# Clustered attention, PReLU FFN and routed experts: output copies, routing steps and attention's first scores put elsewhere

## The chip, the cores and the metric

The kernel runs on one core of one Trainium2 chip. The metric is the device time of one execution in microseconds (us). Five engines work beside each other, each with its own in-order instruction queue: TensorE (matmuls; its weight loads are listed apart), VectorE, ScalarE, GpSimd, and SyncE, which here only issues DMAs. In the rows they are PE (PEld for the weight loads), DVE, ACT, POOL and SP (SPq for SP's issues).

## The reference, cut to what matters

Three stages, all in float32:

```
# attention: batch 2, 8 heads, 768 positions, head size 64, 16 clusters per head
q_assign, k_assign = argmax over clusters of normalised q, k times normalised centroids
scores = where(q_assign == k_assign, q @ k.T / 8, -1e9);  attn = softmax(scores);  x = attn @ v
# FFN on 1536 rows of 512, hidden size 2048
h = x @ w_in;  g = max(h, 0) + alpha * min(h, 0);  y = g @ w_out
# experts: 8 of them, hidden size 1024, rows with y @ w_skip <= 0 pass through
e = argmax(y @ w_gate);  out = y + softmax(y @ w_gate)[e] * (max(y @ w1[e], 0) @ w2[e])
```

## The kernel before

**Precision.** Each float32 operand is held as a high part (a cast to fp32r) and a low part (the rest), and a product is made of three matmuls: high by high, low by high, high by low. So each stage has casts on ScalarE for the high part and subtractions on VectorE or GpSimd for the low part.

**Attention** (`attention`) goes through 8 pairs of heads; each head has 6 steps of 128 query rows, so step i belongs to head i // 6 and pair i // 12, and k = i % 12 is the step within the pair. A step makes 128x768 scores in a PSUM tile `s` (two of them, `ps_s`), takes the maximum (VectorE, `highest`), the exponential (ScalarE, `expo`), the transposes and the product with v two and more steps later. The order of the work in a step is written out by hand (`ORD`), and every engine runs its instructions in that order. The scores are two accumulated matmuls of 128 rows per half: AB holds (q high, q low) stacked on (k high, k high), and CD holds (q high on one-hot cluster rows) on (k low on one-hot rows times 2^60), so that the mask comes out of the same matmul. AB and CD are filled by DMAs from a tile RL, which holds the four parts (1: q high, 2: k high, 0: q low, 3: k low) of both heads of a pair (`place`, L277), and by three DMAs from `st` for the one-hot rows (`placeoh`, L284). For head 0 of pair 0 ScalarE writes the one-hot rows directly into the lower 64 partitions of CD (`onehot0`, L263).

While pair n runs, pair n + 1 is prepared at fixed steps k: similarities (`sims`, L178, at k in SIM = 1, 2), the one-hot tile (`sims2`, at 3), the split into parts (`split`, at k in SP = 2, 3, on GpSimd), `place` at 6, `onehots` and `placeoh` at 8. For pair 1 the scaling of q (`scaleq`, L217) is a ScalarE instruction issued ahead of the loop, directly behind the load of the pair (L441).

At the very start matmuls on a zero tile (`busy`, counts in `WARM`) keep TensorE occupied.

**FFN** (`ffn`) works on two groups of 768 rows, gi 0 and 1 (gi is the batch), and 16 blocks of 128 hidden columns, f 0 to 15. `hiddens` makes a block in two halves c of 384 rows: 12 matmuls into a tile `h` (two buffers, `ps_h`), then PReLU, then the cast `gh` (L656) and the low part `gl` (L658). `second` (L666) multiplies a finished block into six PSUM tiles y of 128 rows; `ps_y` has six banks for the twelve tiles of both groups, so group 1's tile t takes the bank of group 0's tile t once that has been copied out (`evac`, L685: a ScalarE copy and two DMAs). TensorE's order in group 1 is: the two halves of block f, then `second` of block f - 1 for f up to 12; blocks 13 to 15 follow each other directly, and the rest of the second products comes in `tail`.

Blocks 0 and 1 of group 0 are interleaved with the last steps of attention (`blocks`, L727), with `act=True`: ScalarE makes Relu(-h) and Relu(h), VectorE adds them with the slope (L645). In group 1 ScalarE makes Relu(-h) and scales it (L650), and VectorE combines it with h in PSUM (L651). Otherwise VectorE does both (L653, L654).

Weights of the FFN come in as 64-bit words and are converted on ScalarE, VectorE and GpSimd (`Convert.word`), two blocks ahead.

**Routing.** In group 1 VectorE computes group 0's gate products (`gateb`) between the blocks. `route1` (L716: best expert, running counts per expert in `Ms`) stands in block 10, `ranks` (L935: three small matmuls that sum the counts, then positions on VectorE) in block 11, `first_tile` (L959: one-hot of the positions, then six small matmuls into a tile of `ps_h` that give the row numbers of the first expert tile) in blocks 12 and 13, and the gather of these rows behind it. `wsp.hi` and `wsp.lo` split the first experts' weights in chunks.

Of the kernel before, what the change touches and what calls it, by code (L numbers as in the profile page):

```python
# [20 lines left out]
P = 128  # L21
# [65 lines left out]
LK = 8  # L87
XB = 3
LATE = 3
WARM = (8, 3, 4, 9, 14)  # L90
PREP = (33, 45)
OK = 8
PK = 8
# [5 lines left out]
def attention(ctx, tc, A, cst, xs, conv=None, prepare=None, then=None):  # L99
# [192 lines left out]
    grp = {}  # L292
    dens = {}

    def scores(i):
        hd, t = divmod(i, NT)
        n, j = divmod(hd, 2)
        AB, CD = ABs[j], CDs[j]
        s = ps_s.tile([P, 2, 512], F32, tag="s", name="s")
        for u in range(2):  # L300
            ks = slice(u * 384, (u + 1) * 384)
            nc.tensor.matmul(s[:, u, :384], lhsT=AB[:, 0, t * P:(t + 1) * P], rhs=AB[:, 1, ks], start=True, stop=False)  # L302
        for u in range(2):
            ks = slice(u * 384, (u + 1) * 384)
            nc.tensor.matmul(s[:, u, :384], lhsT=CD[:, 0, t * P:(t + 1) * P], rhs=CD[:, 1, ks], start=False, stop=True)  # L305
        if t % 3 == 0:
            if j == 0:
                dens[n, t // 3] = wk.tile([P, 2, 3], F32, tag="den", name="den", bufs=4)
            den = dens[n, t // 3][:, j]
            eth = wk.tile([P, NT, 384], F32R, tag="eth", name="eth", bufs=2)  # L310
            etl = wk.tile([P, NT, 384], F32R, tag="etl", name="etl", bufs=2)
            grp[i // 3] = (den, eth, etl)
        es[i] = s
# [113 lines left out]
    sims(0, 1)  # L427
    busy(WARM[2])
    oq = onehot0(0)
    busy(WARM[3])  # L430
    sims2(0, (1,))
    ok = onehot0(1)
    busy(WARM[4])
    st = heads[0, "st"] = hk.tile([96, 2, 2, P], F32R, tag="st", name="st", bufs=1)
    nc.vector.tensor_copy(st[:, 0], oq[:96, 0])
    nc.vector.tensor_scalar(out=st[:, 1], in0=ok[:96, 1], scalar1=BIG, scalar2=-BIG, op0=ALU.mult, op1=ALU.add)
# [1 line left out]
    vsplit(0, 1)  # L438
    if len(seq) > 1:
        load(1)  # L440
        scaleq(1)  # L441

    def before():
        def new(n):
# [10 lines left out]
    for i in range(NI + L + 7):  # L455
        n, k = divmod(i, 12)
        m = n + 1
        if i == NI and then is not None:
            early.close()
            for _ in first:  # L460
                pass
            fill = then(wk.tile([P, 2 * DM], I32, tag="RL", name="cvt", bufs=1))
            next(fill)
        if conv is not None and i in (2, 3):
            conv.load(i - 2)
        if conv is not None and i in PREP:
            prepare(PREP.index(i))
        if i % 3 == 1 and 0 <= i - 4 < NI and (i - 4) // 3 % 4 > 1:
            recip((i - 4) // 12, (i - 4) // 3 % 2)
        gi, part = divmod(i - L - 3, 3)  # L470
        live = 0 <= gi < NI // 3
        back = 0 <= i - L < NI
        for do in ORD[i % 3]:
            if do == "S" and i < NI:
                scores(i)
            if do == "S" and k == 0 and n < len(seq):
                place(n, 1)
                placeoh(n, 1)
            if do == "M" and i < NI:
                highest(i)  # L480
            if do == "P" and live:
                pv(gi, part)
                if part == 1 and gi % 4 > 1:
                    recip2(gi // 4, gi % 2)
            if do in "AB" and back:
                transp(i - L, "AB".index(do))
            if do in "ab" and back:
                lows["ab".index(do)]()
            if do == "V" and live:
                evac(gi)  # L490
            if do == "E" and i < NI:
                expo(i)
            if do == "X" and conv is not None and CV0 <= i and (k not in CVX or i >= NI):

                next(first, None)
        if live and part == 2 and gi % 4 > 1:
            late.append((i + (LATE if i < NI else 0), gi))
        if late and late[0][0] <= i:
            gl = late.pop(0)[1]
            spare += normalize(gl // 4, gl % 2)  # L500
            while spare and i < NI:
                spare.pop(0)()
        for _ in range(FILL[max(i - NI, 0)] if i >= NI else 0):
            next(fill, None)
            if spare and i > NI + NRM:
                spare.pop(0)()
        if m < len(seq):
            if k in SIM:
                sims(m, SIM.index(k))
            if k == S2 and m == 1:  # L510
                sims2(m)
            if k in SP:
                split(m, SP.index(k))
            if k == S2 and m > 1:
                sims2(m)
            if k == 6:
                place(m, 0)
            if k == OK:
                onehots(m)
            if k == PK:  # L520
                placeoh(m, 0)
            if k == LK and m + 1 < len(seq):
                load(m + 1)
            if k == VS[0]:
                vsplit(m, 0)
            if k == VS[1]:
                vsplit(m, 1)
            if k == 11 and m + 1 < len(seq):
                scaleq(m + 1)
# [51 lines left out]
def ffn(tc, A, cst, xs, xp, y1d, R, cv, W32, fw, ps_h, cvt, more):  # L581
# [42 lines left out]
    def hiddens(gi, f, eng, after=lambda c: None, between=lambda: None, act=False, mid=lambda c: None):  # L624
        xh, xl = xs[gi]
        wh, wl = ws.pop((f, 0))
        if gi == 1 and NF - TAIL <= f < NF - 2:
            gh, gl = over["xh"].pop(0), over["xh"].pop(0)
        else:
            gh = fw.tile([P, GN], F32R, tag="gh", name="gh")  # L630
            gl = fw.tile([P, GN], F32R, tag="gl", name="gl")
        for c in range(2):
            o = slice(c * HC, (c + 1) * HC)
            h = ps_h.tile([P, HC], F32, tag="h", name="h")
            for i, (a, x) in enumerate(((wh, xh), (wh, xl), (wl, xh))):
                for k in range(KD):
                    nc.tensor.matmul(h, lhsT=a[:, k * P:(k + 1) * P], rhs=x[:, k, o], start=(k == 0 and i == 0), stop=(k == KD - 1 and i == 2))  # L637
                if i < 2:
                    yield
            m = fw.tile([P, HC], F32, tag="gm", name="gm")  # L640
            if act:
                t = fw.tile([P, HC], F32, tag="gt", name="gt", bufs=1)
                nc.scalar.activation(t, h, AF.Relu, scale=-1.0)
                nc.scalar.activation(m, h, AF.Relu)
                nc.vector.scalar_tensor_tensor(out=m, in0=t, scalar=nalpha[:, f:f + 1], in1=m, op0=ALU.mult, op1=ALU.add)  # L645
            elif gi == 1:

                t = fw.tile([P, HC], F32, tag="gt", name="gt", bufs=1)
                nc.scalar.activation(t, h, AF.Relu, scale=-1.0)
                nc.scalar.activation(t, t, AF.Copy, scale=nalpha[:, f:f + 1])  # L650
                nc.vector.scalar_tensor_tensor(out=m, in0=h, scalar=0.0, in1=t, op0=ALU.max, op1=ALU.add)  # L651
            else:
                nc.vector.tensor_scalar(out=m, in0=h, scalar1=0.0, scalar2=alpha[:, f:f + 1], op0=ALU.min, op1=ALU.mult)  # L653
                nc.vector.scalar_tensor_tensor(out=m, in0=h, scalar=0.0, in1=m, op0=ALU.max, op1=ALU.add)  # L654
            mid(c)
            nc.scalar.copy(gh[:, o], m)  # L656
            between()
            eng.tensor_tensor(out=gl[:, o], in0=m, in1=gh[:, o].bitcast(F32), op=ALU.subtract)  # L658
            after(c)
            if c == 1:  # L660
                gs[f] = (gh, gl)
            yield
# [119 lines left out]
    for f in range(NF):  # L782
# [2 lines left out]
                split(f + 1, 0, nc.vector)  # L785
            split(f, 1, nc.vector, 1)
        if f == 0:
            for i in range(GT // 2):
                evac(i)

        def after(c):
            if f == 0:
                if c == 0:
                    for i in range(GT // 2, GT):
                        evac(i)
                for _ in range(8):
                    next(consts, None)
                return
# [8 lines left out]
                    fn(*args)  # L807

        hidden(1, f, nc.vector, after, lambda: do(1))
        if 0 < f <= NF - TAIL:  # L810
            second(1, f - 1)
        if f == 1:
# [3 lines left out]
            wsp.even[0] = even(0)  # L816
        if f == 10:
            route1(0, GT)
        elif f == 11:
            route2(0, GT)  # L820
            for c in range(2, NPC):
                wsp.load(0, c)
            ranks(nc, R, wk, ps_h, 0, GT, "h")
        elif f == 12:
            oh = ck.tile([P, GT, P], F16, tag="ct", name="poh0")
            row0 = first_tile(nc, R, oh, wk, ps_h, "h", GT)
            next(row0)
        elif f == 13:
            next(row0)
            gather_rows(nc, xg, y1d[:GN], R["gi0"])  # L830
        for c, i in ((0, f - 6),) if 6 <= f < 10 else ((1, 2 * f - 20), (1, 2 * f - 19)) if f in (10, 11) else ():

            if i == 0:
                slot()
# [805 lines left out]
```

## Time and profile before

| | |
|---|---|
| median of 3 runs | 743.99 us (743.09 to 745.3) |
| the profiled execution's own time | 744.96 us |
| its span, first to last instruction | 743.2 us |
| TensorE busy | 712.3 us, 96% |
| VectorE busy | 572.1 us, 77% |
| ScalarE busy | 475.7 us, 64% |
| GpSimd busy | 365.0 us, 49% |
| mean granted clock of TensorE | 0.993 of full speed |

The profile is of one execution. Matmuls are pipelined, so their listed lengths overlap; a gap on TensorE shows as idle time in square brackets ahead of an instruction, with the engine that ended it. In the span the last attention scores are at 243 and the first hidden matmuls at 247; the FFN's group 1 starts at 391, its hidden blocks end at 513, and its tail and the expert stage follow.

### The profile page before, as it was taken

To read this page: it belongs to the slowest core of one execution; us is meant where nothing else is said; L and a number is where in the kernel's file an instruction comes from. 1 tells how busy PE (TensorE), PEld (TensorE's weight loads), DVE (VectorE), ACT (ScalarE), POOL (GpSimd) and SP (SyncE) were. 2 spreads that over 40 slices of the span, in tenths; PEclk is the share of its full clock that TensorE was granted. 3 is DMA by queue.
4 is the path that set the end of the run, shared out by engine and by line. 5 is a ranking of instruction groups with operands and counts; after the bars stand their busy time and mean duration, and the time that the engine had idled before them with its cause. 6 is when DMAs were issued, how large, how long until landed. Compare 5 with 4: busy or idle time off the path is not lost. (4 is left out here: it accounts for less than half of the span.)

```text
span 743.2 us, 11665 instructions
## 1 busy us (share of the span) xinstructions
PE 712.3 (96%) x4030; PEld 625.6 (84%) x4030; DVE 572.1 (77%) x1102; ACT 475.7 (64%) x914; POOL 365.0 (49%) x302
## 2 busy tenths in 40 slices
PE   8999999999999989999999999998989999999993
PEld 5988989988999878888888989988868888888872
DVE  5989888899988888888856899874478877775731
ACT  5879889797899855454536555556427767565630
POOL 4549769678684576666660000000128837482101
PEclk9999999999999999999999999999999999999997
DMA  7967665874663063334107000151629978685000
GB/s 207 228 164 178 130 152 142 198 183 96 155 136 103 0 227 114 114 133 149 73 0 283 1 1 0 58 169 36 235 63 395 395 263 284 254 290 221 17 10 18
DMA packets 45105, 109.21 MB, mean 147 GB/s; under 512 B 9723, under 2 KB 25531, under 8 KB 39665
## 3 DMA queue, kind: packets, MB, share of 16 engines
q1 hardware_dynamic: 38544, 72.01, 34.8%
q0 software_dynamic: 6496, 36.40, 13.4%
q8 instruction: 34, 0.56, 0.3%
q14 instruction: 31, 0.25, 0.1%
HBM read 74.78 MB, written 10.10 MB: 114 GB/s over the span
## 5 line engine op out<-in xcount | busy, mean ns | idle before, releaser
L339 DVE TENSOR_TENSOR etl<-pt,eth 128x384 fp32r<-128x384 f32 x192 | 101.9, 550 | 17.2 <-ACT eth L338 15.0
L338 ACT CAST eth<-pt 128x384 fp32r<-128x384 f32 x192 | 91.2, 489 | 20.5 <-PE pt L336 20.3
L336 PE MATMUL pt<-ident,e 128*128 128x128 f32 x576 | 93.9, 273 | 0.8 <-DVE etl L339 0.7
L318 DVE TENSOR_REDUCE nm<-s 128x1 f32<-128x768 f32 x96 | 90.6, 945 | 3.3 <-PE s L305 3.0
L1110 POOL DMA_INDIRECT xg<-y1d,gi x16 | 27.5, 1718 | 131.2 <-DVE gi L969 115.0
L325 ACT ACTIVATE e<-s,nm 128x768 f32<-128x768 f32 x96 | 87.6, 913 | 5.8 <-DVE nm L318 5.5
L656 ACT CAST gh<-gm 128x384 fp32r<-128x384 f32 x60 | 30.8, 514 | 85.0 <-DVE gm L654 58.9
L336 PEld LDWEIGHTS pt<-ident,e 128*128 128x128 f32 x576 | 73.2, 140 | 8.9 <-DVE etl L339 2.4
L658 DVE TENSOR_TENSOR gl<-gm,gh 128x384 fp32r<-128x384 f32 x60 | 49.9, 832 | 23.3 <-ACT gh L656 23.3
L354 PE MATMUL px<-etl,vh 128*64 128x384 f32 (+1 forms) x192 | 66.0, 370 | 1.7 <-DVE etl L339 1.6
L1374 DVE TENSOR_TENSOR wl<-raw,wh 128x2048 fp32r<-128x2048 f32 (+2 forms) x28 | 48.8, 1755 | 15.5 <-ACT wh L1370 15.5
L637 PE MATMUL h<-xh,wh 128*128 128x384 f32 x256 | 56.6, 343 | 3.7 <-DVE gm L651 3.1
L637 PE MATMUL h<-xh,wl 128*128 128x384 f32 x256 | 56.9, 343 | 1.5 <-DVE wl L617 1.0
L302 PE MATMUL s<-AB 128*128 128x384 f32 x192 | 57.3, 379 | 0.5
L637 PE MATMUL h<-xl,wh 128*128 128x384 f32 x256 | 55.7, 339 | 0.0
L568 POOL TENSOR_TENSOR pre<-ct,pre 128x512 int32<-128x512 int32 x26 | 37.2, 1450 | 36.3 <-DVE ct L566 36.3
L356 PE MATMUL px<-eth,vh 128*128 128x384 f32 x160 | 54.0, 337 | 0.0
L637 PEld LDWEIGHTS h<-xh,wh 128*128 128x128 f32 x256 | 45.7, 189 | 7.4 <-DVE gm L651 3.5
L1232 POOL DMA_INDIRECT out_dram<-o,si x16 | 22.1, 1381 | 60.4 <-DVE o L1227 27.3
L305 PE MATMUL s<-CD 128*128 128x384 f32 x192 | 49.3, 337 | 1.7 <-DMA CD<-st 1.0
L637 PEld LDWEIGHTS h<-xh,wl 128*128 128x128 f32 x256 | 45.0, 190 | 5.0 <-POOL wl L617 3.7
L1370 ACT CAST wh<-raw 128x2048 fp32r<-128x2048 f32 (+2 forms) x28 | 41.3, 1480 | 11.6 <-PE yo L1141 11.6
(337 smaller groups left out, 1831.3 us busy)
## 6 DMA issues: line engine op xcount, KB each, us to landing
AB<-RL SPq DMA_DIRECT2D x32, 384.0 KB, 5.1
raw<-in_wall_dram SPq DMA_DIRECT2D x12, 1024.0 KB, 8.0
raw<-in_w_in_dram SPq DMA_DIRECT2D x16, 512.0 KB, 4.1
raw<-in_w_out_dram SPq DMA_DIRECT2D x16, 512.0 KB, 4.7
Tp<-in_qkT_dram SPq DMA_DIRECT2D x16, 384.0 KB, 3.7
CD<-RL SPq DMA_DIRECT2D x16, 384.0 KB, 6.4
vt<-in_v_dram SPq DMA_DIRECT2D x8, 384.0 KB, 6.2
y1d<-yb SPq DMA_DIRECT2D x12, 256.0 KB, 3.7
```

Source lines behind the costliest of these rows:

```text
L302: nc.tensor.matmul(s[:, u, :384], lhsT=AB[:, 0, t * P:(t + 1) * P], rhs=AB[:, 1, ks], start=True, stop=False)
L305: nc.tensor.matmul(s[:, u, :384], lhsT=CD[:, 0, t * P:(t + 1) * P], rhs=CD[:, 1, ks], start=False, stop=True)
L318: nc.vector.tensor_reduce(out=nm, in_=s[:, :, :384], axis=AX.XY, op=ALU.max, negate=True)
L325: nc.scalar.activation(e.rearrange("p (u c) -> p u c", u=2), s[:, :, :384], AF.Exp, bias=nm, accum_out=den[:, i % 3:i % 3 + 1])
L336: nc.tensor.transpose(pt[:, i2], e[:, kt * P:(kt + 1) * P], ident)
L338: nc.scalar.copy(eh, pt)
L339: lows[u] = lambda: nc.vector.tensor_tensor(out=etl[:, 3 * u:3 * u + 3, q * P:(q + 1) * P], in0=pt, in1=eh.bitcast(F32), op=ALU.subtract)
L354: nc.tensor.matmul(px[:m], lhsT=vh[:, kt, :m], rhs=etl[:, kt], start=False, stop=False)
L356: nc.tensor.matmul(px, lhsT=vh[:, kt, :], rhs=eth[:, kt], start=False, stop=(kt == NT - 1))
L637: nc.tensor.matmul(h, lhsT=a[:, k * P:(k + 1) * P], rhs=x[:, k, o], start=(k == 0 and i == 0), stop=(k == KD - 1 and i == 2))
L658: eng.tensor_tensor(out=gl[:, o], in0=m, in1=gh[:, o].bitcast(F32), op=ALU.subtract)
L1374: eng.tensor_tensor(out=lo[:, a:b], in0=self.src(t, c)[:, a:b], in1=hi[:, a:b].bitcast(F32), op=ALU.subtract)
```

## The change

- In the FFN, group 0's six output tiles are copied out two ahead of group 1's block 0, one behind each half of block 0 and one behind each half of block 1 (before: three ahead, three behind the first half of block 0).
- `ranks` moves from block 11 to block 10, `first_tile` from 12 to 11, its matmuls from behind block 13 to directly behind block 12's hidden matmuls (ahead of block 11's second product), the gather from 13 to 12; four weight chunks move from blocks 10 and 11 to 11 and 12.
- With `act=True` the PReLU takes the form that group 1 has: ScalarE makes Relu(-h) and scales it, VectorE combines it with h in PSUM.
- The first two attention steps take their three products from RL directly, each a matmul of 64 rows per half (`scores0`), and from CD only the lower 64 partitions (the one-hot rows). `scores0` stands ahead of the second `onehot0`. The two runs of 9 and 14 warm-up matmuls become one of 6 behind it.
- For pair 1 `scaleq` is issued at the end of step 1, and `sims`, `sims2` and `split` come a step later.

```diff
-WARM = (8, 3, 4, 9, 14)
+WARM = (8, 3, 4, 6)
...
+    def scores0(t):
+
+        RL = heads[0][:D]
+        s = es[t] = ps_s.tile([P, 2, 512], F32, tag="s", name="s")
+        for a, b in ((1, 2), (0, 2), (1, 3)):
+            for u in range(2):
+                nc.tensor.matmul(s[:, u, :384], lhsT=RL[:, a, t * P:(t + 1) * P], rhs=RL[:, b, u * 384:(u + 1) * 384], start=(a == 1 and b == 2), stop=False)
+
     def scores(i):
         hd, t = divmod(i, NT)
         n, j = divmod(hd, 2)
         AB, CD = ABs[j], CDs[j]
-        s = ps_s.tile([P, 2, 512], F32, tag="s", name="s")
-        for u in range(2):
+        if i < 2:
+            s = es[i]
+            AB, CD = None, CD[D:]
+        else:
+            s = ps_s.tile([P, 2, 512], F32, tag="s", name="s")
+        for u in range(2) if AB is not None else ():
...
     oq = onehot0(0)
+    sims2(0, (1,))
+    for t in range(2):
+        scores0(t)
+    ok = onehot0(1)
     busy(WARM[3])
-    sims2(0, (1,))
-    ok = onehot0(1)
-    busy(WARM[4])
...
         load(1)
-        scaleq(1)
...
-            if k in SIM:
-                sims(m, SIM.index(k))
-            if k == S2 and m == 1:
+
+            kk = k - (m == 1)
+            if m == 1 and k == 1:
+                scaleq(1)
+            if kk in SIM:
+                sims(m, SIM.index(kk))
+            if kk == S2 and m == 1:
                 sims2(m)
-            if k in SP:
-                split(m, SP.index(k))
-            if k == S2 and m > 1:
+            if kk in SP:
+                split(m, SP.index(kk))
+            if kk == S2 and m > 1:
                 sims2(m)
...
-            if act:
-                t = fw.tile([P, HC], F32, tag="gt", name="gt", bufs=1)
-                nc.scalar.activation(t, h, AF.Relu, scale=-1.0)
-                nc.scalar.activation(m, h, AF.Relu)
-                nc.vector.scalar_tensor_tensor(out=m, in0=t, scalar=nalpha[:, f:f + 1], in1=m, op0=ALU.mult, op1=ALU.add)
-            elif gi == 1:
+            if act or gi == 1:
...
         if f == 0:
-            for i in range(GT // 2):
+            for i in range(2):
                 evac(i)
 
         def after(c):
+            if f < 2:
+                evac(2 + 2 * f + c)
             if f == 0:
-                if c == 0:
-                    for i in range(GT // 2, GT):
-                        evac(i)
                 for _ in range(8):
                     next(consts, None)
                 return
...
         hidden(1, f, nc.vector, after, lambda: do(1))
+        if f == 12:
+            next(row0)
         if 0 < f <= NF - TAIL:
             second(1, f - 1)
...
         if f == 10:
             route1(0, GT)
+            ranks(nc, R, wk, ps_h, 0, GT, "h")
         elif f == 11:
             route2(0, GT)
             for c in range(2, NPC):
                 wsp.load(0, c)
-            ranks(nc, R, wk, ps_h, 0, GT, "h")
-        elif f == 12:
             oh = ck.tile([P, GT, P], F16, tag="ct", name="poh0")
             row0 = first_tile(nc, R, oh, wk, ps_h, "h", GT)
             next(row0)
-        elif f == 13:
-            next(row0)
+        elif f == 12:
             gather_rows(nc, xg, y1d[:GN], R["gi0"])
-        for c, i in ((0, f - 6),) if 6 <= f < 10 else ((1, 2 * f - 20), (1, 2 * f - 19)) if f in (10, 11) else ():
+        for c, i in ((0, f - 6),) if 6 <= f < 10 else ((1, 2 * f - 22), (1, 2 * f - 21)) if f in (11, 12) else ():
```

## Rows read from the trace of the kernel before

**Rows 1.** The page's busy times: engine, us, share of the span, instructions.
```profile
PE 712.3 (96%) x4030; PEld 625.6 (84%) x4030; DVE 572.1 (77%) x1102; ACT 475.7 (64%) x914; POOL 365.0 (49%) x302
```

**Rows 2.** TensorE's waits in the whole span: us in total, times, longest.
```profile
PE h L637 <- DVE gm L651: 3.1, 2, 1.8
```

**Rows 3.** Timeline of TensorE, attention: start, us, line, tiles, idle before and releaser.
```profile
14.96 0.59 PE L305 MATMUL s<-CD 128*128 128x384 f32 x2 [0.66 <-DMA CD<-RL]
...
16.75 1.52 PE L186 MATMUL sim<-bd,Tp 128*128 128x32 f32 x12 [0.50 <-ACT Tp L220]
18.11 0.60 PE L302 MATMUL s<-AB 128*128 128x384 f32 x2
...
40.72 0.59 PE L305 MATMUL s<-CD 128*128 128x384 f32 x2 [1.01 <-DMA CD<-st]
```

**Rows 4.** Timeline of GpSimd and of SP's issues, attention.
```profile
25.18 2.89 POOL L231 TENSOR_TENSOR RL<-Tp,zero 128x768 fp32r<-128x768 f32 x2 [2.31 <-DMA CD<-st]
...
35.45 3.62 SPq L287 DMA_DIRECT2D CD<-st  x3
```

**Rows 5.** DMA issues from 14.9 to 16.45: count, KB each, us to landing.
```profile
CD<-RL SPq DMA_DIRECT2D x1, 384.0 KB, 9.9
```

**Rows 6.** Single lines of the kernel: count, ns shortest/median/longest, first and last start.
```profile
L645 DVE SCALAR_TENSOR_TENSOR gm<-gt,nalpha,gm x4: 918/1366/1643, 254.0 to 266.3; 128x384 f32<-128x384 f32 x4
...
L654 DVE SCALAR_TENSOR_TENSOR gm<-h,gm x28: 557/557/559, 273.3 to 384.2; 128x384 f32<-128x384 f32 x28
...
L644 ACT ACTIVATE gm<-h x4: 482/490/494, 252.8 to 265.2; 128x384 f32<-128x384 f32 x4
...
L650 ACT ACTIVATE gt<-gt,nalpha x32: 614/617/619, 394.2 to 514.9; 128x384 f32<-128x384 f32 x32
```

**Rows 7.** Busy times from 252 to 268: engines; then clock, DMA share, GB/s.
```profile
252.00:268.00 16.00, 14.80 (x76) 12.71 (x74) 15.33 (x19) 9.17 (x22) 13.61 (x13) 1.00 0.12 34
```

**Rows 8.** Timeline of TensorE, first two hidden blocks.
```profile
258.89 0.97 PE L637 MATMUL h<-xh,wh 128*128 128x384 f32 x4 [0.48 <-ACT gm L644]
...
268.94 0.96 PE L637 MATMUL h<-xh,wl 128*128 128x384 f32 x4 [1.03 <-DVE wl L617]
```

**Rows 9.** Timeline of VectorE, group 0, the same instruction of two successive blocks.
```profile
281.15 0.61 DVE L653 TENSOR_SCALAR gm<-h,alpha 128x384 f32<-128x384 f32 x1
...
289.66 0.61 DVE L653 TENSOR_SCALAR gm<-h,alpha 128x384 f32<-128x384 f32 x1
```

**Rows 10.** Timeline of ScalarE and VectorE, group 1, blocks 0 and 1.
```profile
395.86 1.56 ACT L688 COPY yb<-y 128x512 f32<-128x512 f32 x3
...
402.47 0.51 ACT L656 CAST gh<-gm 128x384 fp32r<-128x384 f32 x1 [0.80 <-DVE gm L651]
...
404.72 0.51 ACT L656 CAST gh<-gm 128x384 fp32r<-128x384 f32 x1 [0.69 <-DVE gm L651]
...
397.55 0.43 DVE L1432 TENSOR_TENSOR low<-iota 128x256 bf16<-128x256 f32 x1
```

**Rows 11.** Timeline of TensorE, group 1, block 1.
```profile
399.10 0.97 PE L637 MATMUL h<-xh,wh 128*128 128x384 f32 x4 [1.29 <-DVE gm L651]
...
401.31 1.55 PE L673 MATMUL y<-wh,gh 128*128 128x512 f32 x6
```

**Rows 12.** Timeline of TensorE and VectorE, group 1, blocks 10 and 11.
```profile
471.89 0.87 PE L637 MATMUL h<-xh,wh 128*128 128x384 f32 x4
...
480.19 0.87 PE L637 MATMUL h<-xh,wh 128*128 128x384 f32 x4
...
480.62 1.14 DVE L932 TENSOR_TENSOR Ms<-Ms,M 128x8 bf16<-128x8 bf16 x6
```

**Rows 13.** Timeline of TensorE and ScalarE, block 14; then busy times and clock.
```profile
503.28 1.49 PE L637 MATMUL h<-xh,wh 128*128 128x384 f32 x4 [1.83 <-DVE gm L651]
...
507.29 0.49 ACT L649 ACTIVATE gt<-h 128x384 f32<-128x384 f32 x1 [2.48 <-PE h L637]
...
505.00:506.00 1.00, 1.00 (x5) 1.00 (x4) 0.64 (x2) 0.00 (x0) 1.00 (x1) 0.50 0.00 0
```

## The prediction

> **What bounds the kernel now.** I read the page's first part first: TensorE is busy for 712.3 of 743.2 us, VectorE for 572.1, ScalarE for 475.7 [rows 1]. So the time is TensorE's instruction stream plus the gaps in it; a change wins by closing gaps and loses by opening them. Then the list of TensorE's waits: the longest kind is that for the FFN's hidden tile, 3.1 us in two waits, the longer one 1.8 us [rows 2]. The last view is the timeline of each engine around the four places that the diff touches. The profiled execution took 744.96 us, 1.76 more than its span and 0.97 above the median of the runs shown, 743.99; I work out a difference from the profile and add it to the median.
>
> **Part A, the start of attention.** Removed: 17 warm-up matmuls of 384 columns. Added: 12 score matmuls on 64 rows where the first two steps had 4 on the stacked AB tile, so 8 more; a pair took 0.59 us with its drain [rows 3], so at most 0.3 us each, 2.4 us, and they stand in the stretch that the 17 leave. What goes is the wait of step 0 for the DMA into CD, 0.66 us before 14.96 [rows 3]: the one-hot rows that it now waits for are written by ScalarE. The third step's scores, at 18.11, stood behind the similarities of pair 1, which had waited 0.50 us for the scaling of q and started at 16.75 [rows 3]. Moved a step on, these 1.36 us are put off, not won. TensorE can lead by the idle that goes, 1.16 us at most; I estimate 0.7.
>
> That lead meets a wait that does not move. Step 12 is the first of pair 1; its CD scores started at 40.72 after 1.01 us of idle for the DMA of the one-hot rows [rows 3]. Those three DMAs were issued from 35.45 on, behind the DMAs of the split parts, which wait for GpSimd; and GpSimd's split could start only at 25.18, because its output buffer was still being read by DMAs of pair 0 [rows 4], one of which took 9.9 us to land [rows 5]. The diff moves none of these issues on SP (the load of pair 1 keeps its place, only the scaling behind it moves), and GpSimd's weighting, moved with the similarities, had 2.31 us of idle behind it [rows 4], more than the 1 us or so by which it comes later. So TensorE comes to step 12 earlier and waits longer. I take 0 for part A. Bounds: 1.2 us gained if that DMA chain moves too; 1.6 us lost if the longer wait lowers the clock (price in part C).
>
> **Part B, the first two hidden blocks** (gi 0, f 0 and 1, four halves). Each half loses a Relu on ScalarE (0.490 us) and gains a Copy with scale (0.617), 0.13 more. On VectorE the combining instruction had two SBUF inputs and took 0.92 to 1.64 us, median 1.37; the new one reads the hidden tile in PSUM and one SBUF tile, as line 654 does, whose 28 instructions all took 0.557 to 0.559 [rows 6]. The four took 5.30 us together (the timeline's 1.36, 1.64, 0.92 and 1.38); four at 0.558 take 2.23: 3.07 us less. VectorE is the bound here, 15.33 of 16 us busy from 252 to 268 beside a GpSimd at 13.61 [rows 7], and TensorE waited there 0.48 us for a hidden buffer and 1.03 for a weight half that VectorE splits [rows 8]. The gain does not fade in the blocks after: they repeat every 8.51 us (281.15 to 289.66) on VectorE's own in-order chain [rows 9], above the 8.30 us that the same matmuls take in gi 1 (471.89 to 480.19) [rows 12], so an earlier start of the chain is an earlier end of the stage. Against it: the hidden buffer is now held until VectorE has read it, not only until ScalarE's second read, so the wait of 0.48 us [rows 8] becomes some 0.8; and VectorE will meet GpSimd at other places. I take 2.5 us gained, near the sum; bounds 0.5 (if other stretching on VectorE takes the rest) and 3.1.
>
> **Part C, the output copies spread.** Before, three copies stood ahead of the second half's Relu (1.56 us for three) [rows 10], and TensorE waited 1.29 us for the hidden buffer at 399.10 [rows 11]. With one copy there ScalarE is done about 1 us earlier, but VectorE has constants to write until 397.98 (the last starts at 397.55 and takes 0.43) [rows 10]; its read of the hidden tile then ends at 398.54 (0.557 by line 654 [rows 6]) and TensorE goes on at 398.59: 0.51 us gained.
> Then the copies of y4 and y5 come behind the casts of block 1's two halves. The second product of block 0 comes directly after block 1's hidden matmuls, started at 401.31, and takes a fresh PSUM tile each 0.232 us (six in 1.39 us; the row's 1.55 holds the last one's drain) [rows 11]; its fifth and sixth tiles are the banks of y4 and y5. It would now start at 400.80 and want y4's bank at 401.73 and y5's at 401.96. The cast of the first half started at 402.47, that of the second at 404.72 [rows 10]. I put the first at 402.3 and the copy of y4 behind it from 402.7 to 403.3 (about 0.6 for one, and 0.1 of overlap); this pushes the second half by what slack it lacks, so its cast to 404.9 and the copy of y5 to 405.3 to 405.9. TensorE stands from 401.7 to 403.3 and, after one matmul, from 403.55 to 405.95. The sixth matmul was at 401.31 + 5 x 0.232 = 402.47; it comes 3.5 us later. What follows in this stage is TensorE back to back, so nothing gives it back.
> To this comes the clock. After the wait of 1.83 us at 503.28 the granted clock was 0.50, the level of 1.2 GHz, and a group of four matmuls took 1.49 us [rows 13] against 0.97 at full clock [rows 11]; three such groups make 1.56 us. After the 1.29 us at 399.10 the group took the 0.97. The new stop has 4.0 us of idle with one matmul between, so I add 1.5 us. Part C: 5.0 us lost; bounds 3.5 (no clock loss) and 5.3.
> The Trainium skill's page "TensorE: Matmul & The Clock Gate" (HAM oscillation) shows the clock lowered by waits of about 3 to 5 us between bursts. By it the two gaps of 1.6 and 2.4 us would leave the clock up and part C would cost 3.5; the drop after 1.83 us speaks for the other, and the page's case is the second rival.
>
> **Part D, ranks and row numbers a block ahead.** Before, the row-number matmuls stood in block 13 and took one of two hidden buffers; the next block waited 1.83 us and then ran at half clock, some 3.4 us on TensorE [rows 13]. Now they stand ahead of block 11's second product, which covers them. But then ScalarE's chain of the last three blocks is next late: it had been idle only 2.48 us before 507.29 [rows 13], so no more than 2.5 us come back. And the rank matmuls now stand directly behind block 9's second product, which ended at 480.19, while the counts that they sum were finished by VectorE at 481.76 (480.62 + 1.14) [rows 12]. Everything on TensorE queues behind them: 1.6 us of new wait. The row-number matmuls wait in turn for VectorE to read block 12's first hidden tile, which I put 0.2 us late, and take 0.15. Net: 2.5 - 1.6 - 0.35 = 0.6 us gained. Bounds: 1.5 gained (3.4 - 1.9, if ScalarE does not hold it up); 1.0 lost, if the 1.6 us wait lowers the clock (1.56). Moving weight chunks by a block I cost at nothing: their readers come in the expert stage, after 513; without that cover it would be two casts, 1.2 us.
>
> **Sum.** A 0, B -2.5, C +5.0, D -0.6: +1.9, so 743.99 + 1.9 = 745.9 us.
>
> **Rivals.**
> 1. *The rank wait drops the clock too* (slower). For it: 1.6 us of idle is near the 1.83 that did it; against it: 1.29 us did not. It decides from the point where 1.6 us is enough. D becomes +1.0, the sum 743.99 + 3.5 = 747.5.
> 2. *The clock holds through the stop at the copies.* For it: two gaps, neither far above 1.83; against it: that wait. C is 3.5, the sum 744.4.
> 3. *VectorE's saving is swallowed* by its other two-input instructions beside GpSimd or by the longer-held hidden buffer. For it: the spread of 0.92 to 1.64 us [rows 6] shows how much such meetings move; against it: the fixed 8.51 us period. B is -0.5, the sum 747.9.
> 4. *Every part at its best end*: the head start survives, the clock holds, ScalarE does not bind. A -1.2, B -3.1, C +3.5, D -1.5: -2.3, 741.7. Against it: four things at once.
>
> **How the numbers follow.** A difference of 0.3%, 2.2 us, is about what a measurement can tell from none: below 741.8 is faster, above 746.2 slower. Chances: forecast 0.44 (a third of it above 746.2), rival 1 0.15, rival 2 0.20, rival 3 0.11, rival 4 0.10. Slower: 0.14 + 0.15 + 0.11 = 0.40; faster: rival 4, 0.10; same 0.50. Range: from 742.4, short of rival 4, to 749.2, which takes in rivals 1 and 3 and most of their sum.
>
> **What would show it.** A: step 12's CD scores still start near 40.7. B: line 651 at 0.56 us in the first blocks, and the stretch from step 12 to the start of gi 1 2 to 3 us shorter. C: waits of TensorE of 1.6 and 2.4 us for the copies at line 688 in block 1 of gi 1, and a lower clock after them. D: a wait of the rank matmuls for the counts of 1.6 us, and no wait of 1.83 us in block 14. If no wait for the copies shows in block 1, the forecast is wrong and the kernel is faster.

## The result and the profile after

The change makes the kernel slower: 754.06 us, median of ten runs (750.66 to 758.5), against 743.88 (742.78 to 749.26), a ratio of 1.0121 with a 95% interval of 1.0101 to 1.0142. Forecast were 745.9 and at most 749.2. The profiled execution shown here took 758.5 us, with a span of 756.7; it is the longest of the ten, so its marks say more for the attention start than the median does. Below, a loss or gain of a run in us is the difference of two medians, and the interval belongs to the ratio beside it. An execution more than 1.5% above the fastest of its kernel counts as slow and is left out of the ratio (one of the twelve in run 3).

The page's busy times of the kernel after (columns as in [rows 1]):

```profile
PE 725.8 (96%) x4021; PEld 637.9 (84%) x4021; DVE 571.3 (75%) x1102; ACT 476.5 (63%) x914; POOL 363.6 (48%) x302
```

TensorE is busy 13.5 us longer than in [rows 1], and the span is 13.5 us longer. So the loss is not one of new gaps on balance: the same kind of instructions take longer. Four marks on TensorE's timeline place it. First hidden matmul of the FFN: 247.19 before, 257.55 after (+10.36). First of group 1: 391.37 before, 400.06 after (+8.69, so the first blocks won 1.67). First of block 2 of group 1: 405.43 before, 419.93 after (+14.50, so the copies cost 5.81). First of the tail: 513.47 before, 527.15 after (+13.68, so ranks and row numbers won 0.82).

**Attention.** Timeline of TensorE before, ahead of what [rows 3] shows:

```profile
5.16 2.76 PE L186 MATMUL sim<-bd,Tp 128*128 128x32 f32 x24
...
9.53 0.31 PE L249 MATMUL po<-identb,oh 128*96 128x128 bf16 x2 [0.95 <-DVE oh L211]
9.68 1.63 PE L140 MATMUL warm<-warm 128*128 128x384 bf16 x9
...
11.51 2.44 PE L140 MATMUL warm<-warm 128*128 128x384 bf16 x14
```

The same after, and a window with the granted clock (us, PE busy, clock, DMA share, GB/s):

```profile
5.06 5.17 PE L186 MATMUL sim<-bd,Tp 128*128 128x32 f32 x24
...
11.30 0.42 PE L249 MATMUL po<-identb,oh 128*96 128x128 bf16 x2
11.65 4.21 PE L301 MATMUL s<-RL 64*128 64x384 f32 x12
...
16.03 2.13 PE L140 MATMUL warm<-warm 128*128 128x384 bf16 x6
...
21.16 1.01 PE L314 MATMUL s<-AB 128*128 128x384 f32 x2 [1.44 <-ACT e L337]
...
23.89 2.61 PE L186 MATMUL sim<-bd,Tp 128*128 128x32 f32 x12
...
33.98 0.99 PE L314 MATMUL s<-AB 128*128 128x384 f32 x2
...
37.51 0.59 PE L314 MATMUL s<-AB 128*128 128x384 f32 x2
...
50.70 0.51 PE L317 MATMUL s<-CD 128*128 128x384 f32 x2
```

```profile
32.00:36.00 4.00, 4.00 (x18) 1.00 0.00 0
```

A pair of score matmuls takes 1.01 at 21.16 and 0.99 at 33.98, but 0.59 at 37.51, as in [rows 3]; twelve similarities take 2.61 where [rows 3] has 1.52. By these durations TensorE works at the lower level, 1.2 GHz, from the start to about 37, though it has no gap after 21.16: a pair takes 1.01 in run 8 too, where the clock column shows 0.50. Here the column shows 1.00 even from 32 to 36, so it misses the level. The wait of 1.44 ahead of step 2 stands where the similarities used to be; step 12 (50.70) waits for no DMA any more.

Not all of the 10.36 us is the change's. Up to the transposes of the one-hot rows TensorE's instructions are the same in both kernels, and these started at 11.30 and not at 9.53, since the similarities ahead of them took 5.17 us and not 2.76. The level at this point differs between executions: the four warm-up matmuls behind the similarities take 0.81 us in four of the fourteen profiles of this document, that of the kernel before among them, and 1.25 to 1.47 in the other ten, with the old start and the new. So some 1.8 us of this comparison lie ahead of anything that the change touches. What the change can alter is when the level comes up behind that point.

**First hidden blocks.** VectorE's line 662 (line 651 before), then TensorE's two waits:

```profile
264.35 0.54 DVE L662 SCALAR_TENSOR_TENSOR gm<-h,gt 128x384 f32<-128x384 f32 x1
```

```profile
269.88 0.97 PE L653 MATMUL h<-xh,wh 128*128 128x384 f32 x4 [1.12 <-DVE gm L662]
...
286.70 0.98 PE L653 MATMUL h<-xh,wl 128*128 128x384 f32 x4 [0.62 <-POOL wl L633]
```

VectorE takes 0.54 to 0.56 us in place of the 0.92 to 1.64 of [rows 6]. Between the marks at 247.19 and 391.37 TensorE waited 3.19 us before: the 0.48 and 1.03 of [rows 8], 0.59 for ScalarE's `xb`, and two more:

```profile
262.57 0.96 PE L673 MATMUL y<-wh,gh 128*128 128x512 f32 x3 [0.63 <-ACT xb L371]
...
278.00 0.98 PE L637 MATMUL h<-xh,wl 128*128 128x384 f32 x4 [0.46 <-POOL wl L617]
```

After, it is 2.35 us: the two above and 0.61 for `xb`. The wait for a weight half of GpSimd stands in block 3 both times.

The shorter VectorE instruction agrees with what the Trainium skill's page "SBUF — State Buffer" (Who interferes with whom) says: a VectorE instruction with both inputs in SBUF contends with GpSimd's reads, and the new form has one input in PSUM. The kernel before shows the contention in the low part `gl` too, which has both inputs in SBUF: 1.09 and 1.41 us beside a busy GpSimd, but 0.55 at 262.14, where GpSimd stood idle until 263.11.

```profile
256.75 1.09 DVE L658 TENSOR_TENSOR gl<-gm,gh 128x384 fp32r<-128x384 f32 x1
...
262.14 0.55 DVE L658 TENSOR_TENSOR gl<-gm,gh 128x384 fp32r<-128x384 f32 x1
...
263.11 1.86 POOL L568 TENSOR_TENSOR w32b<-cvt,w32b 128x256 int32<-128x256 int32 x2 [1.24 <-DVE cvt L566]
```

**Copies.** TensorE in block 1 of group 1, and a window (us, PE busy, granted clock, DMA share, GB/s); compare [rows 10, 11]:

```profile
407.19 0.98 PE L653 MATMUL h<-xh,wh 128*128 128x384 f32 x4 [0.68 <-DVE gm L662]
...
409.40 1.09 PE L684 MATMUL y<-wh,gh 128*128 128x512 f32 x4
411.92 0.49 PE L684 MATMUL y<-wh,gh 128*128 128x512 f32 x1 [1.43 <-ACT yb L699]
414.58 0.80 PE L684 MATMUL y<-wh,gh 128*128 128x512 f32 x1 [2.17 <-ACT yb L699]
415.17 2.76 PE L684 MATMUL y<-wl,gh 128*128 128x512 f32 x6
```

```profile
415.00:420.00 5.00, 5.00 (x14) 0.55 0.91 279
```

The four matmuls that have a bank run, then one waits for each copy, and then six matmuls take 2.76, where six of these products took 1.55 in [rows 11].

**Ranks and row numbers.** TensorE after, the starts of blocks 10 and 11, then block 12 and block 15; compare [rows 12, 13]:

```profile
486.38 0.87 PE L653 MATMUL h<-xh,wh 128*128 128x384 f32 x4
...
495.12 0.18 PE L950 MATMUL rk<-M,tri 128*128 128x48 bf16 x1 [0.27 <-DVE M L900]
496.10 0.18 PE L951 MATMUL rk<-Ms,ones 128*128 128x48 bf16 x1 [0.80 <-DVE Ms L942]
...
496.32 0.95 PE L653 MATMUL h<-xh,wh 128*128 128x384 f32 x4
...
508.91 0.30 PE L978 MATMUL sv<-rs,poh 128*128 128x1 f16 x6
...
522.79 0.97 PE L653 MATMUL h<-xh,wh 128*128 128x384 f32 x4 [0.83 <-DVE gm L662]
```

The wait of 1.83 us and the half clock behind it [rows 13] are gone. The rank matmuls wait 0.27 and 0.80, and block 11 starts 9.94 us behind block 10, where it was 8.30 [rows 12]: 1.64 us later. The clock was 1.00 from 496 to 500.

### The profile page after: what moved, and what is told of

Same layout as the page of the kernel before. It is cut to its first block, busy times and chain, and to the rows that moved or that the text cites. A ratio compares the mean times of both kernels' runs of the same rounds, so it can differ in the third digit from the quotient of the medians.

```text
span 756.7 us, 11646 instructions
## 1 busy us (share of the span) xinstructions
PE 725.8 (96%) x4021; PEld 637.9 (84%) x4021; DVE 571.3 (75%) x1102; ACT 476.5 (63%) x914; POOL 363.6 (48%) x302
## 5 line engine op out<-in xcount | busy, mean ns | idle before, releaser
L348 PE MATMUL pt<-ident,e 128*128 128x128 f32 x576 | 96.3, 278 | 1.1 <-DVE etl L351 0.8
L348 PEld LDWEIGHTS pt<-ident,e 128*128 128x128 f32 x576 | 75.1, 143 | 9.8 <-DVE etl L351 3.0
L317 PE MATMUL s<-CD 128*128 128x384 f32 (+1 forms) x192 | 51.0, 349 | 0.0
```

Of the source, the lines that this page charges most:

```text
L348: nc.tensor.transpose(pt[:, i2], e[:, kt * P:(kt + 1) * P], ident)
```

## The experiments

The open question was the start: the kernel after loses there what the prediction put at nothing. Runs 1 to 4 ask whether the thin warm-up makes it. In the expectations of runs 5 to 9 theory R is that matmuls on 64 partitions let the clock fall, S that the late similarities do, B that only both together with the thin warm-up do.

**1. The change without the attention start** (its five hunks left out; all else as changed).

> The changed kernel with attention's start as before (parts B, C and D only). If the loss sits in attention's start (theory 1, the clock comes up late, and its rivals 2 and 3 there), what is left is B, C and D: by the changed kernel's trace -1.7, +5.8 and -0.8, so about +3.3 us against the kernel before, 747, and executions close together. If the loss were spread over the kernel, it stays near +10.

748.71 us, ratio 1.0037 (1.0018 to 1.0056). More than half of the loss is the start; the rest is here, and the marks give it as -1.67, +5.81 and -0.82 = +3.3, the difference of 3.3 us to 745.42, the median of the kernel before on that chip. In the profile of this run, with the old start, the first 24 similarities take 5.17 us as well.

**2. The attention start alone.**

> The kernel before with attention's new start alone (part A). All theories that place the rest of the loss here: +6 to +7 us in the median, single executions from +3 to +11, and a trace in which TensorE's early matmuls run at half speed (two score matmuls 0.99 us instead of 0.60) for some stretch before step 12. The forecast's part A said 0.

751.82 us, ratio 1.0069 (1.0041 to 1.0096): 6.4 us lost (3.1 to 7.2 by the interval). With run 1 that makes 9.7 of the 10.2 us, so within the intervals the parts add. TensorE in this profile:

```profile
9.37 0.31 PE L249 MATMUL po<-identb,oh 128*96 128x128 bf16 x2 [0.97 <-DVE oh L211]
9.61 2.59 PE L301 MATMUL s<-RL 64*128 64x384 f32 x12
12.12 0.45 PE L249 MATMUL po<-identb,oh 128*96 128x128 bf16 x2
```

The new scores begin at the upper level and the level falls while they run, without a gap: the same transposes take 0.31 ahead of them and 0.45 behind. The granted clock is 0.50 from 12 to 24.

**3. The same, with all the warm-up matmuls kept.**

```
-WARM = (8, 3, 4, 6)
+WARM = (8, 3, 4, 14, 9)
...
     oq = onehot0(0)
+    busy(WARM[4])
```

> Part A alone, but with the 9 and the 14 warm-up matmuls kept (9 ahead of the early scores, 14 behind the second one-hot transposes). Theory 1 (too little warm-up work leaves TensorE at 1.2 GHz): the loss goes, within 1 us of the kernel before, no half-speed stretch after 17. Rival 2 (the 64-row matmuls keep the clock low, however much warm-up stands around them): still +4 or more, with half-speed rows. Rival 3 (the similarities and the split a step later make pair 1 late): still +4 or more, but at full speed, with TensorE waiting at step 12.

747.89 us (746.02 to 757.39), ratio 1.0032 (1.0004 to 1.0061): 2.5 us lost. None of the three forecasts came: more warm-up seems to help, but does not bring the time back. The profile is of the longest execution, 757.39; there the clock was 0.50 from 28 to 36, and a pair of scores took 0.99 as late as 36.74.

**4. The kernel before with the thin warm-up.**

```
-WARM = (8, 3, 4, 9, 14)
+WARM = (8, 3, 4, 0, 6)
```

> The kernel before with only its warm-up thinned: none instead of 9, and 6 instead of 14; scores and similarities as before. Theory 1: slower, +3 to +8 us, spread between executions, half-speed rows in some profile. Rivals 2 and 3: no change (within 0.5 us), since the warm-up covers idle time only.

745.26 us, ratio 0.9989 (0.997 to 1.0008): nothing lost. Fewer warm-up matmuls alone don't do it.

**5. Only the second pair's similarities and scaling a step later** (the last two attention hunks alone).

> Only the second pair's scaling of q and similarities come a step later; scores of the first two steps on the stacked tile and all warm-up matmuls stay. Theory S (the late similarities open an idle stretch of about 1.4 us ahead of step 2, where TensorE waits for ScalarE's exponentials, and the clock falls there and comes back late): 2 to 6 us more than before, 746 to 750, with the granted clock at 0.50 somewhere in 18 to 37. Theory R (the 12 matmuls on 64 rows let the clock fall): within 1 us of before, 743 to 745, clock up from about 13 on. Theory B (only both together with the thin warm-up): within 1.5 us of before.

745.0 us, ratio 0.9992 (0.9979 to 1.0004). The shift by itself costs nothing, so theory S falls as the whole account. The same wait ahead of step 2 is there, and here the clock stays up:

```profile
18.62 0.61 PE L302 MATMUL s<-AB 128*128 128x384 f32 x2 [1.38 <-ACT e L325]
...
20.24 1.52 PE L186 MATMUL sim<-bd,Tp 128*128 128x32 f32 x12
...
41.97 0.59 PE L305 MATMUL s<-CD 128*128 128x384 f32 x2 [0.92 <-DMA CD<-st]
```

**6. Only the new scores, with the thin warm-up** (the other attention hunks alone).

> The other half of the attention start: scores of the first two steps from the unstacked parts on 64 rows, with the short warm-up of 6, but the second pair's scaling and similarities at their old places. Theory S: the similarities fill the time ahead of step 2 again, so about the time before, 743 to 746, with full clock by about 21. Theory R: nearly all of the start's loss is here, 748 to 752, with half clock far beyond 21. Theory B: 743 to 746.

748.05 us, ratio 1.0028 (1.0007 to 1.0049): 2.5 us lost, at the lower edge of what R gave, and with a wide spread, 743.86 to 751.77. The scores lose by themselves, the shift does not, and together they lose 6.4. So the shift seems to cost where the scores are on 64 partitions; but the intervals of run 6 (0.5 to 3.7 us) and run 2 (3.1 to 7.2) touch, and that is likely rather than shown.

**7. The attention start alone, scores on 128 partitions.**

```
-        RL = heads[0][:D]
+        RL = heads[0]
```

> The whole new attention start alone, but its 12 score matmuls contract all 128 partitions of the parts and not 64: same number, same columns, same places (the scores of the first two steps become the sum over two heads, so the output is not the reference's). Theory R: the clock stays up or comes up by about 13, time 744 to 747. Theory S and theory B: nothing changes against the start alone, 749 to 753, half clock in 12 to 24 or longer.

745.59 us, level with the kernel before, ratio 0.9997 (0.998 to 1.0015), against 751.82 in run 2. Number of matmuls, columns, places, warm-up and the late similarities are those of run 2. The start:

```profile
11.58 3.05 PE L301 MATMUL s<-RL 128*128 128x384 f32 x12
...
14.58 1.14 PE L140 MATMUL warm<-warm 128*128 128x384 bf16 x6
...
18.67 0.62 PE L314 MATMUL s<-AB 128*128 128x384 f32 x2 [1.73 <-ACT e L337]
...
22.86 0.99 PE L314 MATMUL s<-AB 128*128 128x384 f32 x2
```

They begin at the lower level like those of the kernel after, but the level rises while they run: the twelve take 3.05 where the kernel after took 4.21, and six warm-up matmuls 1.14 where it took 2.13. The level does not hold in this profile, though, which is of the longest of the twelve executions (749.22): it falls again behind the wait of 1.73 us ahead of step 2, to a granted clock of 0.50 from 20 to 24. So the stop of theory S can lower the clock in single executions, with full-height scores too; the median shows no cost of it, and in run 9's profile the same wait, 1.71 us, left the clock up.

**8. The kernel before, its last 23 warm-up matmuls on 64 partitions.**

```
-    busy(WARM[3])
+    busy(WARM[3], D)
...
-    busy(WARM[4])
+    busy(WARM[4], D)
```

(`busy` then takes its operands from `warm[:64]`.)

> The kernel before, and nothing changed but the 9 and the 14 warm-up matmuls of the start, which contract 64 partitions and not 128; number, columns and places are the same and their product is not read by anything. Theory R (work on 64 rows does not hold or lift the clock as work on 128 does): half clock reaches past 20 us in the profile, and the time is 1 to 5 us above before, 746 to 750. Rival (rows do not matter; the 128-row scores won by something else): as before, 744.5 to 746. The thin warm-up, which lacks the 9, cost nothing, so a time as before would not settle it alone; the clock's rows would.

749.34 us, ratio 1.0051 (1.003 to 1.0072): 4.2 us lost by rows alone, in a kernel that has none of the change. TensorE, then windows with the granted clock:

```profile
9.68 3.06 PE L140 MATMUL warm<-warm 64*128 64x384 bf16 x9
...
13.04 4.66 PE L140 MATMUL warm<-warm 64*128 64x384 bf16 x14
17.63 1.01 PE L302 MATMUL s<-AB 128*128 128x384 f32 x2
...
22.21 0.59 PE L302 MATMUL s<-AB 128*128 128x384 f32 x2
```

```profile
8.00:12.00 4.00, 3.66 (x14) 0.50 0.94 193
12.00:16.00 4.00, 4.00 (x15) 0.50 1.01 280
16.00:20.00 4.00, 4.00 (x13) 0.50 0.98 236
20.00:24.00 4.00, 4.00 (x28) 0.80 1.06 213
```

The nine and the fourteen take 3.06 and 4.66 where the kernel before took 1.63 and 2.44. From 9.68 to 17.6 TensorE has hardly a gap and stays at 0.50; the clock comes up between 20 and 24, behind the first scores on 128 partitions.

**9. The whole change, scores on 128 partitions** (the edit of run 7).

> The whole change, with the 12 score matmuls of the first two steps contracting all 128 partitions and not 64 (the scores of these two steps become the sum over two heads, so the output is not the reference's). Theory R (rows are what the attention start costs; the other three parts add): the time of the change with the old start, 748 to 749.5, 5 to 6 us below the whole change. Rival (with the other parts the start's loss is of another kind, the late similarities' idle): 751 to 755.

748.44 us, ratio 1.0047 (1.0026 to 1.0067): 5.6 us below the kernel after, and level with run 1. With this one slice put back to full height, the new attention start costs nothing beside the old one.

**10. The change without the attention start and without the copies.**

> The change without the new attention start and without the spread output copies: the first hidden blocks' form and the ranks and row numbers a block ahead. Prediction's theory of the copies (3.5 of stall and 1.5 of clock, measured 5.8 by the marks in the trace): 5 to 6 us below the kernel with the old start, so 742.5 to 744, and no wait for the copies in block 1. Rival (the copies only show a stop that the earlier blocks would give elsewhere): 745.5 to 748.

743.38 us, ratio 0.9972 (0.9956 to 0.9988): 1.8 us won. Run 1, which has the copies, lost 3.3; so they cost 5.1 us. Where run 1 waited 1.45 and 2.16 us for the copies, TensorE now has only the wait of old, and its six products take 1.55:

```profile
397.18 0.96 PE L637 MATMUL h<-xh,wh 128*128 128x384 f32 x4 [1.28 <-DVE gm L646]
...
399.39 1.55 PE L668 MATMUL y<-wh,gh 128*128 128x512 f32 x6
```

**11. The parts that won, and the copies kept in block 0.** Old start; copies 2 ahead of block 0, 1 behind its first half, 3 behind its second; ranks in block 11 as before, row numbers behind them and behind block 12's hidden tile; the first blocks' form, the gather and the weight chunks as in the change. Cut to the copies and the row-number matmuls:

```
-            for i in range(GT // 2):
+            for i in range(2):
                 evac(i)
...
-                if c == 0:
-                    for i in range(GT // 2, GT):
-                        evac(i)
+                for i in (2,) if c == 0 else range(3, GT):
+                    evac(i)
...
         hidden(1, f, nc.vector, after, lambda: do(1))
+        if f == 12:
+            next(row0)
```

> Old attention start; the VectorE form of the first two hidden blocks; output copies 2, 1 and 3 around the halves of block 0, so that none is left for block 1; rank matmuls in block 11 as before, row numbers behind them and in block 12. Theory (the terms as measured in the traces: first blocks -1.7, copies -0.5 to -1.3 with no wait for the banks, half-clock stretch at 503 gone -1.5 to -2.4 with no wait for the counts): 738.5 to 741, and no wait of TensorE for the copies. Rival (each stop merely moves: three copies behind the second half hold up block 1, or row numbers in block 11 stop TensorE as they did in block 13): 743 to 746.

744.91 us, ratio 0.9987 (0.9968 to 1.0006): no difference that can be told, as the rival had it. The copies wait for nothing (TensorE waits 0.68 for the hidden tile where it waited 1.29), but the row numbers now stop TensorE, since VectorE comes to block 12's hidden tile behind the whole chain of ranks:

```profile
492.87 0.29 PE L962 MATMUL sv<-rs,poh 128*128 128x1 f16 x6 [2.17 <-DVE gm L646]
```

**12. The same, the rank matmuls between block 11's hidden tile and the second product behind it.**

```
         hidden(1, f, nc.vector, after, lambda: do(1))
-        if f == 12:
+        if f == 11:
+            ranks(nc, R, wk, ps_h, 0, GT, "h")
+        elif f == 12:
             next(row0)
...
-            ranks(nc, R, wk, ps_h, 0, GT, "h")
             oh = ck.tile([P, GT, P], F16, tag="ct", name="poh0")
```

> The kernel before with the VectorE form of the first two hidden blocks, the output copies 2, 1 and 3 in block 0, and the rank matmuls of block 11 moved to right behind its hidden tile, ahead of the second product, row numbers behind block 12's hidden tile. Theory (every stop is covered by a second product of 4.4 us): no wait for the counts, no wait of 2.2 us for the row numbers as in the kernel with parts kept, the stage's end 3 to 4 us earlier than before; 740.5 to 743, ratio below 0.9985. Rival (the stop comes back elsewhere, ScalarE's chain in the last blocks is late by as much): 743.5 to 746, as the kernel with parts kept.

742.69 us (741.54 to 745.47), ratio 0.9957 (0.9937 to 0.9977): 2.5 us below the kernel before (745.15), the lowest median here. Its interval overlaps that of run 10, so which of the two is faster is not shown.

```profile
482.17 0.20 PE L935 MATMUL rk<-M,tri 128*128 128x48 bf16 x1
...
492.20 0.29 PE L963 MATMUL sv<-rs,poh 128*128 128x1 f16 x6 [1.42 <-DVE gm L646]
...
510.47 1.78 PE L676 MATMUL y<-more 128*128 128x512 f32 x7
```

The ranks wait for nothing, the row numbers still 1.42 us; the tail starts 3.0 us earlier than before (513.47), from a start of the FFN (247.23) that is the same within 0.1 us. The span is 1.9 us shorter (741.3 against 743.2).

## Why the prediction was wrong

**Part A: wrong, and it alone takes the time out of the range.** The step that failed is "I take 0 for part A", and in it "at most 0.3 us each, 2.4 us, and they stand in the stretch that the 17 leave". The added matmuls were priced by their duration at full clock. The clock was thought of for waits alone, and in part A only for the one at step 12. Runs 7 and 8 show the price: the same matmuls on 128 partitions cost nothing, and 64-partition matmuls in the old kernel's warm-up cost 4.2 us. The whole part measured +6.4 in run 2, and the bounds had gone to +1.6. That warm-up matmuls were removed was not it by itself (run 4), nor were the late similarities (run 5); on top of the new scores each of the two seems to add (run 2 against runs 3 and 6).
The estimated lead of 0.7 us failed too: with the similarities moved on, TensorE waits ahead of step 2 for ScalarE's exponentials, 1.38 us in run 5 and 1.44 in the kernel after.
The zero itself had a reason, the DMA chain ahead of step 12. With the scores on 128 partitions a zero comes out: run 7 gives no loss and no gain, run 9 is level with run 1, and in run 5 step 12's wait for the DMA stands, at 41.97. In the kernel after the chain can't be tested, since TensorE is later than it. The interplay (2.5 for the scores, about 0 for the shift, 6.4 together) is likely, and how it comes about is not shown: why the kernel after still runs at 1.2 GHz from 21.16 to 37, on work of 128 partitions and without a gap, is open.

**Part B: right, smaller.** The VectorE instruction takes 0.56 as the prediction said. Won were 1.67 us of the 2.5 forecast: the wait for the hidden buffer became 1.12 and not 0.8, and the wait for a weight half of GpSimd, 0.46 before and not in the sum, stayed and is 0.62.

**Part C: right.** Waits of 1.43 and 2.17 at the fifth and sixth product stand for the forecast 1.6 and 2.4, and the clock fell as forecast; 5.1 us by runs 1 and 10, 5.8 by the marks, for the 5.0. Rival 2 falls: its two gaps did lower the clock, to 0.55 from 415 to 420. The Trainium skill's page "TensorE: Matmul & The Clock Gate" (HAM oscillation) shows the clock lowered by waits of about 3 to 5 us; in this trace shorter ones did it.

**Part D: right.** -0.82 by the marks for the forecast -0.6: the ranks cost 1.64 by the start of block 11 (1.6 forecast), the row numbers wait for nothing and cost 0.16 (0.35), and 2.6 came back (2.5). What kept it from more was ScalarE's chain, as forecast: the wait of 0.83 at 522.79 is for VectorE, which had waited for ScalarE. Rival 1 falls, the clock held. Rival 3 did not come: 1.67 us of VectorE's 3.07 arrived, not 0.5.

B, C and D together were forecast at +1.9 and measured +3.3 in run 1. The rest is A.

## What to carry to other kernels

Before a full-height matmul is replaced by several on half the partitions, ask what the clock does there, above all near the start or behind a stop: the price was not the 0.3 us of each matmul but several microseconds of everything behind them at 1.2 GHz. Test such a step by filling the partitions, with number and columns kept. And put a small matmul that waits for another engine behind a long run of matmuls that gives that engine its time (run 12), and a copy that frees a bank ahead of the block that wants the bank.

## What was not expected of the hardware

- TensorE can be without a gap and yet stay at the lower level. In run 8 it ran 23 matmuls on 64 partitions from 9.68 to 17.6 at a granted clock of 0.50. The Trainium skill's page "TensorE: Matmul & The Clock Gate" (What's actually happening) says that the clock is set by how busy the engine has been; here the engine was busy and the clock stayed low.
- A wait of 1.38 us at full clock left the clock up (run 5, 18.62), two waits of 1.43 and 2.17 us with one matmul between them did not (411.92 to 414.58). Behind nearly the same wait ahead of step 2 the clock fell in run 7 (1.73 us) and not in run 9 (1.71), so the length of a wait does not settle it alone.
- The clock column of the page can miss the level. The kernel after shows 1.00 throughout its first 40 us, but its first 24 similarities took 5.17 us, against 2.76 in the profile of the kernel before, whose column shows 1.00 too. For the start, durations of equal instructions are the surer sign.
- The start differs from run to run of one kernel: run 6 spreads over 7.9 us, and the kernel before over 742.66 to 749.05 in the runs beside runs 1 to 4.
